# A third arm for experts with 129 to 192 tokens, and another PSUM pool for the third block's transposes

## The chip, the cores and the metric

The kernel runs on one core of one Trainium2 chip. The metric is the device time of one execution in microseconds (us). Before the change it is 526.41 us, the median of three runs (525.23 to 527.89).

## The reference

Three layers follow each other on 1536 tokens of width 512 in float32.

1. Chunked local attention (2 batches, 8 heads, 768 positions, chunks of 32, 8 memory keys).
2. A dense layer pair, `h = x @ w_in`, `g = h * sigmoid(1.702 * h)`, `g @ w_out`, with 2048 inner columns.
3. A mixture of 8 experts, which is the part that the change touches:

```python
logits = x @ w_gate
expert_idx = np.argmax(logits, axis=1)
...
h = np.maximum(np.einsum('ecd,edf->ecf', disp, w1), 0.0)
y = np.einsum('ecf,efd->ecd', h, w2)
...
        out[i] = gate_w[i] * y[expert_idx[i], pos[i]]
```

Each expert has `w1` (512 x 1024) and `w2` (1024 x 512) and takes at most 384 tokens. How many tokens an expert gets depends on the data. With the drawn inputs the experts, in the order in which the kernel takes them, get 224, 291, 128, 160, 128, 256, 160 and 189 tokens; the text calls them expert 0 to expert 7.

## The kernel before

**Precision.** A float32 operand is kept as two numbers, high and low, that TensorE takes at its fast float32 rate (`F32R`). A product is three matmuls: high by high, high by low, low by high. So a weight tile has a high and a low half (`w[:, 0]`, `w[:, 1]`), and activations `xs` and `hT` have too. ScalarE (ACT) writes the high half with a copy, VectorE (DVE) the low half with a subtraction. The weights of the next expert are widened in this way while an expert is computed: a piece is ACT L295 and then DVE L300.

**Control flow.** The program holds all code for every expert one after the other, and branches on the token count in registers; every engine runs the branches for itself. Expert e (from 1 on) goes like this, in `others`:

- The first arm (`both(cnt > P, ...)`, P is 128): `first_of_two` for more than 128 tokens, with the weights stationary and the 256 columns of two token blocks moving, 8 chunks (`fc`) of 12 matmuls in L879; or `first_of(0)` for one block (L962, L971). Both hold the transposes of the next expert's tokens (`next_trans`, L846).
- `thirds_first`: for more than 256 tokens the first layer of a third block, for up to 64 rows in `small_h` (transposes L906, then L918 and L925). All paths hold the first 6 matmuls of layer 2 (`start2`).
- `after_arms`: layer 2 of block 0 (L1002, 24 matmuls with those of `start2`).
- `second`: layer 2 of block 1, either all of it (L1002) or, for up to 192 tokens, `small2` (L940, 16 matmuls on the 64 tokens left, which GpSimd has copied into `hT["pair"]`, L1056); or `second_not`, one small matmul (L1018).

So in the trace 96 matmuls of L879, 24 of L1002 and 16 of L940 in this order are an expert with 129 to 192 tokens. In the code an arm that isn't taken still stands between the others and is jumped over (the branch instructions have the line L1064).

**PSUM.** `psum(kind, name)` takes a buffer from a pool: "t" has 2 buffers, "h" has 4 in the expert stage, and they are reused in turn. A chunk of `first_of_two` takes one "h" buffer, which is free again when DVE has read it (L883).

Of the kernel before, what the change touches and what calls it, by code (L numbers as in the profile page):

```python
# [9 lines left out]
F32 = mybir.dt.float32  # L10
# [5 lines left out]
AF = mybir.ActivationFunctionType  # L16
ALU = mybir.AluOpType
# [4 lines left out]
P = 128  # L22
# [12 lines left out]
PUMPS = (1, 3, 5)  # L35
# [6 lines left out]
KEEPS = (3, 7, 8)  # L42
HALF = P // 2
# [5 lines left out]
TFC = 5  # L49
# [43 lines left out]
def kernel(  # L93
# [14 lines left out]
    nc = tc.nc  # L108
    NT, DM = out.shape
    NG, _, NPAIR, KW = k.shape  # L110
# [3 lines left out]
    E, _, F = w1.shape  # L114
# [5 lines left out]
    KC = DM // P  # L120
# [226 lines left out]
    def w_next(e, keep=KEEP):  # L347

        name, i = (flight[0].name, flight[0].i) if flight else pieces[min(w_at[0], w_end[0] - 1)][:2]
        if not flight or name[1] * 8 + 4 * (name[0] == "w2") + 2 * name[2] + i >= 8 * e + 8 + keep:  # L350
            return False
        w_step()
        w_loads(8 * F // 512)
        return True
# [22 lines left out]
    def w_tile(name, i):  # L377
        while (name, i) not in ready:
            assert flight or wide or w_can_load(), name
            w_pump()  # L380
        return where[name].rearrange("p z (c f) -> p z c f", f=512)
# [22 lines left out]
    def psum(kind, name):  # L404
        pool, tag, shape = ps_pools[kind]
        return pool.tile(shape, F32, tag=tag, name=name)
# [409 lines left out]
    def expert_parts(e, ep, tp, cnt):  # L816
# [15 lines left out]
        def xs_of(b):  # L832

            if b in own:
                return own[b], 0
            i = min(b, 2)
            key = 0 if i < 2 else b
            if key not in xs:
                xs[key] = ep.tile([P, 2, KC, 2 * P if i < 2 else P], F32R, tag="xs" if i < 2 else "xst",
                                  name="xs", bufs=2 if i < 2 else 1)  # L840
            return xs[key], (b * P if i < 2 else 0)

        def trans(b):
            ps = psum("t", "pst")
            for c in range(KC):
                nc.tensor.transpose(ps[:, c * P:(c + 1) * P], xr[b][:, c * P:(c + 1) * P], ident)  # L846
            t, o = xs_of(b)
            hi, lo = t[:, 0, :, o:o + P], t[:, 1, :, o:o + P]
            pv = ps.rearrange("p (c n) -> p c n", n=P)
            act = nc.scalar.activation(out=hi, in_=pv, func=AF.Copy)  # L850
            dve = nc.vector.tensor_tensor(out=lo, in0=pv, in1=hi.bitcast(F32), op=ALU.subtract)
            return act.ins, dve.ins
# [9 lines left out]
        def hT_of(b):  # L862
            key = 0 if b < 2 else b
            if key not in hT:
                hT[key] = ep.tile([P, 2, F2, 2 * P if b < 2 else P], F32R, tag="hT" if b < 2 else "hTt", name="hT", bufs=1)
            return hT[key]
# [32 lines left out]
        def small_h(b):  # L899

            x = narrow(xs_of(b)[0])
            h = narrow(hT_of(b))
            with in_order():
                ps = psum("t", "pst")
                for c in range(KC):
                    nc.tensor.transpose(ps[:, c * HALF:(c + 1) * HALF], xr[b][:HALF, c * P:(c + 1) * P], ident[:HALF, :HALF])  # L906
                pv = ps[:, :KC * HALF].rearrange("p (c n) -> p c n", n=HALF)
                nc.scalar.activation(out=x[:, :, 0], in_=pv, func=AF.Copy)
                nc.vector.tensor_tensor(out=x[:, :, 1], in0=pv, in1=x[:, :, 0].bitcast(F32), op=ALU.subtract)
                start2()  # L910
                hs = []
                for j in range(2):
                    w_tile(("w1", e, j), 0)
                    w = w_tile(("w1", e, j), 1)
                    ps = psum("h", "psh")
                    for wz in range(2):
                        for c in range(KC):
                            nc.tensor.matmul(ps, lhsT=x[:, c].rearrange("p z n -> p (z n)"), rhs=w[:, wz, c, :],  # L918
                                             start=(wz, c) == (0, 0), stop=(wz, c) == (1, KC - 1))
                    hs.append(ep.tile([P, 512], F32, tag="hs", name="hs", bufs=2))  # L920
                    nc.scalar.activation(out=hs[j], in_=ps, func=AF.Copy)
                for j in range(2):
                    ps = psum("h", "psu")
                    for c in range(KC):
                        nc.tensor.matmul(ps[:, c * HALF:(c + 1) * HALF], lhsT=hs[j][:, c * P:(c + 1) * P], rhs=pair,  # L925
                                         start=True, stop=True)
                    hi, lo = (h[:, 4 * j:4 * j + 4, z] for z in range(2))
                    pv = ps[:, :KC * HALF].rearrange("p (c n) -> p c n", n=HALF)
                    nc.scalar.activation(out=hi, in_=pv, func=AF.Relu)
                    nc.vector.scalar_tensor_tensor(out=lo, in0=pv, scalar=0.0, in1=hi.bitcast(F32),  # L930
                                                   op0=ALU.max, op1=ALU.subtract)
# [92 lines left out]
        def next_trans():  # L1024
            if e + 1 < E:
                parts[e + 1].trans(0)
                parts[e + 1].trans(1)

        def steps(part):
            while w_next(e, KEEPS[part]):  # L1030
                pass
# [5 lines left out]
        def first_of(b):  # L1037

            with in_order():
                turn = block_h(b, pump_one)  # L1040
                next_trans()
                turn()
                steps(0)

        def first_of_two():

            for b in range(2, NCB):
                load(b)
            for fc in range(F2):
                mm, act = layer1(fc)  # L1050
                if fc == TFC:
                    after_mm = mm
                if fc in PUMPS:
                    w_next(e, KEEPS[0])
            for z in range(2):
                nc.gpsimd.tensor_copy(hT["pair"][:, :, z], hT_of(0)[:, z, :, P:P + HALF])  # L1056
            with tc.issue_after(after_mm):
                next_trans()
            steps(0)

        def both(cond, yes, no):

            before = w_state()
            with tc.If(cond) as some:  # L1064
                yes()
            after = w_state()
            w_back(before)
            with some.Else():
                no()
            assert w_state() == after  # L1070

        def wide_h(b):
            trans(b)
            start2()
            block_h(b)()

# [72 lines left out]

        def others():  # L1150

            both(cnt[ex] > P, first_of_two, lambda: first_of(0))
            thirds_first()
            after_arms()
            y_of(1)
            both(cnt[ex] > P, second, second_not)
# [308 lines left out]
```

## Time and profile before

| what | value |
|---|---|
| median of three runs | 526.41 us |
| the profiled execution, its own time | 525.63 us |
| its span in the trace | 523.8 us |
| PE (TensorE matmul) busy | 507.5 us, 97% of the span |
| DVE, ACT, POOL (GpSimd) busy | 60%, 52%, 23% |
| share of PE in the chain that ended last | 86% |
| instructions in the trace | 10850, of these 4185 matmuls |
| queue q8, kind instruction | 46 packets, 0.75 MB |
| mean granted TensorE clock | 0.992 |

Times in the trace count from the start of the span. The expert stage takes the last 170 us. A row of the timeline gives start, length, engine, line, operation, output and inputs, how many instructions are merged, and in brackets how long the engine was idle before it and what ended the wait. PEld is the weight load that goes with every matmul; PEldq is the sequencer that hands PE its instructions.

### The profile page before, as it was taken

To read this page: it belongs to the slowest core of one execution; us is meant where nothing else is said; L and a number is where in the kernel's file an instruction comes from. 1 tells how busy PE (TensorE), PEld (TensorE's weight loads), DVE (VectorE), ACT (ScalarE), POOL (GpSimd) and SP (SyncE) were. 2 spreads that over 40 slices of the span, in tenths; PEclk is the share of its full clock that TensorE was granted. 3 is DMA by queue.
4 is the path that set the end of the run, shared out by engine and by line. 5 is a ranking of instruction groups with operands and counts; after the bars stand their busy time and mean duration, and the time that the engine had idled before them with its cause. 6 is when DMAs were issued, how large, how long until landed. Compare 5 with 4: busy or idle time off the path is not lost.

```text
span 523.8 us, 10850 instructions
## 1 busy us (share of the span) xinstructions
PE 507.5 (97%) x4185; PEld 437.7 (84%) x4185; DVE 312.1 (60%) x609; ACT 273.5 (52%) x549; POOL 119.5 (23%) x115
## 2 busy tenths in 40 slices
PE   8899999999999999999999999999999999999994
PEld 3689789889989989989988888778888897889893
DVE  4999894588893283232247444638643976964721
ACT  2798986856662263222255223439553955764520
POOL 3334442333520031000000000053202522521121
PEclk9899999999999999999999999999999999999998
DMA  8898655041440004000048511369734897894010
GB/s 331 291 318 295 205 186 179 1 147 59 167 159 35 0 3 161 0 1 1 0 122 270 173 42 61 124 193 391 284 114 154 253 337 253 297 315 171 25 28 30
DMA packets 38994, 80.90 MB, mean 154 GB/s; under 512 B 3913, under 2 KB 10057, under 8 KB 38922
## 3 DMA queue, kind: packets, MB, share of 16 engines
q1 hardware_dynamic: 36010, 70.66, 39.4%
q0 software_dynamic: 2912, 9.27, 5.5%
q8 instruction: 46, 0.75, 0.6%
q14 instruction: 26, 0.21, 0.1%
HBM read 70.43 MB, written 9.75 MB: 153 GB/s over the span
## 4 chain that ended last, share of the span: by engine, by line
PE 86%; DVE 3%; ACT 3%; issue 3%; DMA 2%; POOL 1%; another core or an unknown queue 0%; SPq 0%; POOLq 0%; DVEq 0%; ACTq 0%
PE acc L590 25%; PE psh L547 25%; PE psy L1002 9%; PE psh L879 9%; PE psh L962 3%; PE pse L505 2%; PE psy L940 2%; PE pss L435 1%; DVE w L300 1%; DMA kt<-in_k_dram 1%; PE psy L779 1%; PE pst L846 1%; PE psr L615 1%; PE psh L763 1%; ACT w L295 1%
## 5 line engine op out<-in xcount | busy, mean ns | idle before, releaser
L547 PEld LDWEIGHTS psh<-xT,w 128*128 128x128 f32 x1152 | 146.9, 188 | 8.8 <-ACT g L566 0.7
L590 PE MATMUL acc<-w,g 128*128 128x512 f32 x576 | 153.0, 400 | 0.0
L547 PE MATMUL psh<-xT,w 128*128 128x256 f32 x1152 | 151.9, 281 | 0.4 <-DVE xT L520 0.2
L590 PEld LDWEIGHTS acc<-w,g 128*128 128x128 f32 x576 | 100.7, 188 | 19.4 <-issue 2.1
L562 ACT ACTIVATE sg<-psh 128x256 f32<-128x256 f32 x96 | 36.8, 384 | 127.7 <-PE psh L547 126.1
L300 DVE TENSOR_TENSOR w<-raw,w 128x1024 fp32r<-128x1024 f32 x64 | 76.1, 1221 | 22.9 <-ACT w L295 20.7
L570 DVE TENSOR_TENSOR g<-sg,g 128x256 fp32r<-128x256 f32 x78 | 37.9, 487 | 80.9 <-ACT g L566 76.7
L295 ACT ACTIVATE w<-raw 128x1024 fp32r<-128x1024 f32 x64 | 65.2, 1055 | 2.3 <-ACTq L1064 1.7
L879 PE MATMUL psh<-xs,w 128*128 128x256 f32 x480 | 58.8, 283 | 0.3 <-DVE hT L883 0.2
L1002 PE MATMUL psy<-w,hT 128*128 128x512 f32 x240 | 57.8, 397 | 0.8 <-ACT xs L850 0.7
L879 PEld LDWEIGHTS psh<-xs,w 128*128 128x128 f32 x480 | 57.6, 189 | 0.9 <-DVE hT L883 0.7
L1002 PEld LDWEIGHTS psy<-w,hT 128*128 128x128 f32 x240 | 44.5, 188 | 11.3 <-issue 1.6
L601 DVE SCALAR_TENSOR_TENSOR x<-acc,x 128x512 f32<-128x512 f32 x36 | 24.1, 685 | 20.8 <-PE acc L590 20.8
L566 ACT ACTIVATE g<-psh 128x256 fp32r<-128x256 f32 x96 | 36.4, 380 | 0.0
L827 POOL DMA_INDIRECT xr<-rows,taker x21 | 29.2, 1391 | 17.8 <-ACTq L1064 10.0
L882 ACT ACTIVATE hT<-psh 128x256 fp32r<-128x256 f32 x40 | 15.0, 382 | 31.6 <-PE psh L879 31.5
L725 POOL DMA_INDIRECT y<-rows,taker x1 | 1.2, 1224 | 123.8 <-DVE cnt_i L732 123.8
L883 DVE SCALAR_TENSOR_TENSOR hT<-psh,hT 128x256 fp32r<-128x256 f32 x40 | 16.2, 420 | 21.1 <-ACT hT L882 21.0
L300 POOL TENSOR_TENSOR w<-w,w 128x512 fp32r<-128x512 f32 x12 | 16.9, 1416 | 42.0 <-ACT w L295 42.0
L290 POOL TENSOR_TENSOR w<-w,rest 128x512 int32<-128x512 int32 x13 | 17.4, 1339 | 35.3 <-DVE w L276 33.6
L295 ACT ACTIVATE w<-w 128x512 fp32r<-128x512 f32 x32 | 19.8, 628 | 9.8 <-POOL w L290 5.0
L276 DVE SCALAR_TENSOR_TENSOR w<-raw,w 128x512 int32<-128x512 int32 x32 | 24.6, 775 | 0.3
(155 smaller groups left out, 568.3 us busy)
## 6 DMA issues: line engine op xcount, KB each, us to landing
raw<-in_w_dram SPq DMA_DIRECT2D x64, 512.0 KB, 6.7
raw<-in_w_out_dram SPq DMA_DIRECT2D x16, 512.0 KB, 4.4
raw<-in_w_in_dram SPq DMA_DIRECT2D x16, 512.0 KB, 3.9
vt<-in_v_dram SPq DMA_DIRECT2D x12, 512.0 KB, 4.7
kt<-in_k_dram SPq DMA_DIRECT2D x12, 368.0 KB, 5.7
qt<-in_q_dram SPq DMA_DIRECT2D x12, 256.0 KB, 5.4
out_dram<-blank SPq DMA_DIRECT2D x12, 256.0 KB, 2.7
rows<-x SPq DMA_DIRECT2D x5, 520.0 KB, 4.8
```

The lines of the kernel that those rows point to most:

```text
L276: nc.vector.scalar_tensor_tensor(out=self.w, in0=self.words()[1], scalar=-0x40000000, in1=self.w, op0=ALU.bitwise_and, op1=ALU.bitwise_or)
L295: nc.scalar.activation(out=w_dst(self.name, self.i, 0), in_=w, func=AF.Copy)
L300: eng.tensor_tensor(out=lo, in0=w, in1=hi.bitcast(F32), op=ALU.subtract)
L547: nc.tensor.matmul(ps, lhsT=w[:, wz, c, i * P:(i + 1) * P], rhs=xT[tb][:, xz, c, :], start=n == 0, stop=n == 3 * KC - 1)
L562: nc.scalar.activation(out=sg_t[u], in_=h_t[u], func=AF.Silu, scale=1.702)
L566: g_last[:1] = [nc.scalar.activation(out=g[:, 0], in_=h_t.pop(u), func=AF.Silu, scale=1.702).ins]
L570: lo = eng.tensor_tensor(out=g[:, 1], in0=sg_t.pop(u), in1=g[:, 0].bitcast(F32), op=ALU.subtract)
L590: nc.tensor.matmul(acc_t[tb][s], lhsT=g[:, gz, s * P:(s + 1) * P], rhs=w[:, wz, wi, :], start=i == 0 and n == 0, stop=u == last_of(k, tb) ...
L601: nc.vector.scalar_tensor_tensor(out=dst, in0=acc_t[tb][s], scalar=1 / 1.702, in1=dst, op0=ALU.mult, op1=ALU.add)
L827: return nc.gpsimd.indirect_dma_start(out=t, out_offset=None, in_=rows[:, :], in_offset=bass.IndirectOffsetOnAxis(ap=taker[:, b, ex:ex + 1 ...
L879: mm = nc.tensor.matmul(ps, lhsT=w[:, wz, c, f0:f0 + P], rhs=t[:, xz, c, :], start=m == 0, stop=m == 3 * KC - 1)
L1002: nc.tensor.matmul(ps, lhsT=h[:, hz, fc, o:o + P], rhs=w[:, wz, fc % 4, :], start=fc == 0 and n == 0, stop=fc == F2 - 1 and n == 2)
```

## The change

A new arm, `first_of_narrow`, is taken for 129 to 192 tokens. Since such an expert has at most 192 rows, the high and the low activations of 192 tokens stand side by side as 384 moving columns: for each chunk and each of 4 contraction blocks one matmul of 384 columns multiplies both by the high weights, and one of 256 columns adds high activations by low weights. That is 64 matmuls in place of 96. (The columns from 192 on of the second one fall on the low part; these rows are rows of zeros there.) The eviction has four steps where there were two: ACT copies the low part, DVE adds the high part, ACT takes the relu, DVE subtracts. `first_of_two` remains for more than 192 tokens, and `first_of(0)` for up to 128, behind a second comparison.

The second edit concerns the transposes of a third block: `small_h` and `wide_h` take their PSUM buffer from "h", no longer from "t".

```diff
--- before.py
+++ after.py
@@ -840,8 +840,8 @@
                                   name="xs", bufs=2 if i < 2 else 1)
             return xs[key], (b * P if i < 2 else 0)
 
-        def trans(b):
-            ps = psum("t", "pst")
+        def trans(b, kind="t"):
+            ps = psum(kind, "pst")
             for c in range(KC):
                 nc.tensor.transpose(ps[:, c * P:(c + 1) * P], xr[b][:, c * P:(c + 1) * P], ident)
             t, o = xs_of(b)
@@ -901,7 +901,7 @@
             x = narrow(xs_of(b)[0])
             h = narrow(hT_of(b))
             with in_order():
-                ps = psum("t", "pst")
+                ps = psum("h", "pst")
                 for c in range(KC):
                     nc.tensor.transpose(ps[:, c * HALF:(c + 1) * HALF], xr[b][:HALF, c * P:(c + 1) * P], ident[:HALF, :HALF])
                 pv = ps[:, :KC * HALF].rearrange("p (c n) -> p c n", n=HALF)
@@ -1052,6 +1052,35 @@
                     after_mm = mm
                 if fc in PUMPS:
                     w_next(e, KEEPS[0])
+            with tc.issue_after(after_mm):
+                next_trans()
+            steps(0)
+
+        def first_of_narrow():
+
+            t, _ = xs_of(0)
+            h = hT_of(0)
+            n = P + HALF
+            for fc in range(F2):
+                w_tile(("w1", e, fc // 4), 0)
+                w = w_tile(("w1", e, fc // 4), 1)
+                f0 = (fc % 4) * P
+                ps = psum("h", "psh")
+                for c in range(KC):
+                    nc.tensor.matmul(ps[:, :2 * n].rearrange("p (z n) -> p z n", z=2), lhsT=w[:, 0, c, f0:f0 + P],
+                                     rhs=t[:, :, c, :n], start=c == 0, stop=False)
+                    mm = nc.tensor.matmul(ps[:, :2 * P], lhsT=w[:, 1, c, f0:f0 + P], rhs=t[:, 0, c, :],
+                                          start=False, stop=c == KC - 1)
+                low = ep.tile([P, 512], F32, tag="hs", name="low", bufs=2)[:, :n]
+                nc.scalar.activation(out=low, in_=ps[:, n:2 * n], func=AF.Copy)
+                nc.vector.tensor_tensor(out=low, in0=ps[:, :n], in1=low, op=ALU.add)
+                nc.scalar.activation(out=h[:, 0, fc, :n], in_=low, func=AF.Relu)
+                nc.vector.scalar_tensor_tensor(out=h[:, 1, fc, :n], in0=low, scalar=0.0, in1=h[:, 0, fc, :n].bitcast(F32),
+                                               op0=ALU.max, op1=ALU.subtract)
+                if fc == TFC:
+                    after_mm = mm.ins
+                if fc in PUMPS:
+                    w_next(e, KEEPS[0])
             for z in range(2):
                 nc.gpsimd.tensor_copy(hT["pair"][:, :, z], hT_of(0)[:, z, :, P:P + HALF])
             with tc.issue_after(after_mm):
@@ -1070,7 +1099,7 @@
             assert w_state() == after
 
         def wide_h(b):
-            trans(b)
+            trans(b, "h")
             start2()
             block_h(b)()
 
@@ -1149,7 +1178,8 @@
 
         def others():
 
-            both(cnt[ex] > P, first_of_two, lambda: first_of(0))
+            both(cnt[ex] > P + HALF, first_of_two,
+                 lambda: both(cnt[ex] > P, first_of_narrow, lambda: first_of(0)))
             thirds_first()
             after_arms()
             y_of(1)
```

What the program of an engine holds now is shown by the order of its instructions, at three places. The first is PE, expert 3 (160 tokens), from the end of expert 2 on; `psh` is a chunk's PSUM buffer, `w_97` and `w_96` the two tiles of `w1`, `xs` the activations. Before:

```order
L1064 UNCONDITIONAL_BRANCH
L1018 LDWEIGHTS ones
L1018 MATMUL psy<-ones 32x8
L1064 UNCONDITIONAL_BRANCH
L1064 COMPARE_AND_BRANCH
L879 MATMUL psh<-xs,w_97 128x256 x48
L879 MATMUL psh<-xs,w_96 128x256 x48
L846 MATMUL pst<-ident,xr 128x128 x8
L1064 UNCONDITIONAL_BRANCH
```

And now, with the first of the 64 rows of the new arm (384 and 256 columns in turn):

```order
L1093 COMPARE_AND_BRANCH
L879 MATMUL psh<-xs,w_97 128x256 x48
L879 MATMUL psh<-xs,w_96 128x256 x48
L846 MATMUL pst<-ident,xr 128x128 x8
L1093 UNCONDITIONAL_BRANCH
L1093 COMPARE_AND_BRANCH
L1070 MATMUL psh<-xs,w_97 128x384
L1072 MATMUL psh<-xs,w_97 128x256
```

Where expert 3 fell through one comparison into L879, it now jumps over 104 matmuls to a second comparison and falls into the new arm there.

The second place is the end of that arm, again on PE, where the arm of 128 tokens begins. Now:

```order
L1070 MATMUL psh<-xs,w_96 128x384
L1072 MATMUL psh<-xs,w_96 128x256
L846 MATMUL pst<-ident,xr 128x128 x8
L1093 UNCONDITIONAL_BRANCH
L962 MATMUL psh<-w_97,xs 128x512 x12
L962 MATMUL psh<-w_96,xs 128x512 x6
L971 MATMUL psu<-ident,hs 128x128 x4
L962 MATMUL psh<-w_96,xs 128x512 x6
L846 MATMUL pst<-ident,xr 128x128 x8
L971 MATMUL psu<-ident,hs 128x128 x4
L1093 UNCONDITIONAL_BRANCH
L1093 COMPARE_AND_BRANCH x2
```

The 72 matmuls of the new arm stand between `first_of_two` and `first_of`, in each of the experts 1 to 7 (64 in expert 7, which has no transposes): an expert with 128 tokens makes two jumps in a row at its start, and one with more than 192 jumps further at the end of its arm.

The third place is DVE in the new arm; `low` is the buffer of the added halves, L300 a piece of the next expert's weights:

```order
L1093 COMPARE_AND_BRANCH
L300 TENSOR_TENSOR w_94<-raw_0_3362,w_94 128x1024
L300 TENSOR_TENSOR w_94<-raw_1_3363,w_94 128x1024
L1076 TENSOR_TENSOR low<-psh,low 128x192 x2
L300 TENSOR_TENSOR w_4519<-raw_2_3364,w_4519 128x1024
L1078 SCALAR_TENSOR_TENSOR hT<-low,hT 128x192 x2
L1076 TENSOR_TENSOR low<-psh,low 128x192 x2
L1078 SCALAR_TENSOR_TENSOR hT<-low,hT 128x192 x2
```

Where L883 stood once for a chunk, an addition and a subtraction stand now, in pairs of chunks, and the addition is what frees the PSUM buffer.

## Rows read from the trace of the kernel before

**Rows 1.** The page, parts 1 and 2: the span and PE.

```profile
span 523.8 us, 10850 instructions
...
PE 507.5 (97%) x4185; PEld 437.7 (84%) x4185; DVE 312.1 (60%) x609; ACT 273.5 (52%) x549; POOL 119.5 (23%) x115
```

**Rows 2.** Timeline of PE in the expert stage, experts 2 to 6.

```profile
399.49 4.35 PE L962 MATMUL psh<-w,xs 128*128 128x512 f32 x18
...
412.90 5.96 PE L879 MATMUL psh<-xs,w 128*128 128x256 f32 x48
419.06 5.96 PE L879 MATMUL psh<-xs,w 128*128 128x256 f32 x48 [0.20 <-DVE hT L883]
...
431.31 3.89 PE L940 MATMUL psy<-w,hp 128*128 128x512 f32 x16
435.82 4.41 PE L962 MATMUL psh<-w,xs 128*128 128x512 f32 x18 [0.62 <-issue]
...
463.00 11.27 PE L1002 MATMUL psy<-w,hT 128*128 128x512 f32 x48 [0.70 <-ACT xs L850]
...
474.31 11.66 PE L879 MATMUL psh<-xs,w 128*128 128x256 f32 x96
485.80 1.04 PE L846 MATMUL pst<-ident,xr 128*128 128x128 f32 x8
486.59 5.82 PE L1002 MATMUL psy<-w,hT 128*128 128x512 f32 x24
492.26 3.89 PE L940 MATMUL psy<-w,hp 128*128 128x512 f32 x16
```

**Rows 3.** Timeline of DVE at the start of expert 3.

```profile
411.77 6.90 DVE L300 TENSOR_TENSOR w<-raw,w 128x1024 fp32r<-128x1024 f32 x6 [0.27 <-DVEq L1064]
...
418.59 0.75 DVE L883 SCALAR_TENSOR_TENSOR hT<-psh,hT 128x256 fp32r<-128x256 f32 x2
```

**Rows 4.** Branches by line, whole and in four windows: count, min/median/max ns, first to last.

```profile
L1064 PEldq COMPARE_BRANCH  x43: 65/190/4550, 357.6 to 512.6; - x43
...
L1064 PEldq COMPARE_BRANCH  x2: 179/1862/3546, 395.3 to 395.6; - x2
...
L1064 PEldq COMPARE_BRANCH  x3: 181/318/4550, 430.0 to 431.1; - x3
...
L1064 PEldq COMPARE_BRANCH  x2: 187/1284/2380, 460.1 to 460.3; - x2
...
L1064 PEldq COMPARE_BRANCH  x1: 326/326/326, 505.5 to 505.5; - x1
```

**Rows 5.** The page, part 3: the queue that loads code (packets, MB, share).

```profile
q8 instruction: 46, 0.75, 0.6%
```

**Rows 6.** Windows: 208.8 to 337.9, from one packet of q8 to the seventh after.

```profile
208.80:337.90 129.10, 128.96 (x891) 111.58 (x889) 53.51 (x154) 44.04 (x109) 1.22 (x1) 1.00 0.25 81
```

**Rows 7.** DMA queues in 433.2 to 433.3, 439 to 439.1, 506.6 to 506.7: packets begun.

```profile
q8 instruction: 1, 0.02, 58.8%
...
q8 instruction: 1, 0.02, 62.9%
...
q8 instruction: 1, 0.02, 85.6%
```

**Rows 8.** Windows: span, busy by engine (PE, PEld, DVE, ACT, POOL), clock, DMA share, GB/s.

```profile
430.00:439.00 9.00, 8.38 (x37) 6.50 (x36) 5.76 (x8) 2.70 (x6) 1.18 (x1) 1.00 0.95 328
453.00:465.00 12.00, 11.19 (x85) 10.43 (x85) 8.57 (x14) 6.61 (x15) 4.42 (x5) 1.00 1.01 377
478.00:512.00 34.00, 34.00 (x232) 31.39 (x231) 17.85 (x33) 13.46 (x30) 7.13 (x9) 1.00 0.12 36
```

**Rows 9.** Timeline of expert 1, start of its third block.

```profile
377.98 0.43 PE L906 MATMUL pst<-ident,xr 64*128 64x64 f32 x4 [1.17 <-DVE xs L851]
...
379.80 0.42 DVE L909 TENSOR_TENSOR xs<-pst,xs 128x256 fp32r<-128x256 f32 x1
...
380.27 3.99 PE L918 MATMUL psh<-w,xs 128*128 128x512 f32 x16 [0.28 <-DVE xs L909]
```

## The prediction, made before the changed kernel ran

> **What bounds the kernel now.** I read the page first: PE is busy for 507.5 of 523.8 us [rows 1], so what happens to PE's work, or to its few gaps, sets the time. The profiled execution took 525.63 us, 0.8 below the median of the runs (526.41); sums are made against 525.63 and carried over to the median. A difference under 0.5% (2.6 us) can't be told from none, since the three runs of the kernel before lie 2.7 us apart.
>
> Then I read PE's timeline in the expert stage. Three experts have 96 matmuls of L879, 24 of L1002 and 16 of L940 (experts 3, 6 and 7; the rows show 3 and 6) and will take the new arm [rows 2]. Experts 1 and 5 keep the wide arm, 2 and 4 the arm of 128. PE is idle there in only three places: 0.20 us before the second half of expert 3's chunks, 0.62 at the start of expert 4, 0.70 in expert 5 [rows 2].
>
> Who ends these waits decides the forecast, so I looked at PE's sequencer. Of 43 branches half take 0.19 us or less [rows 4], but four take 2.4 to 4.6: in expert 2's start 3.55, in expert 4's start 4.55, in expert 5 at 460.3 2.38 [rows 4], and a fourth in expert 4, of 3.04, that no row here shows. The second and third end just before PE's idle times of 0.62 and 0.70: 431.1 + 4.55 is 435.7, and PE begins at 435.82; 460.3 + 2.38 is 462.7, and PE begins at 463.00 [rows 2, 4]. So the 0.70 that the timeline puts down to ACT L850 was a jump.
>
> These four wait for code. Queue q8 brings 46 packets [rows 5]; over 7 of them PE ran 891 matmuls and 889 weight loads, 254 instructions a packet [rows 6]. So code comes in blocks of about 256 instructions. For the jump in expert 4's start a packet begins at 433.2, and PE's sequencer goes on at 435.7, 2.4 us later [rows 4, 7]. The next packet begins at 439.0 [rows 7], 3.4 us after the sequencer has come into that block. So a block is asked for when the one before it is entered, and can be run 3.4 + 2.4 = 5.8 us later. With idle DMA queues it is faster: the branch at 505.5 ends at 505.8, a packet begins at 506.6 [rows 4, 7], so 0.8 + 2.4 = 3.2 us. The DMA engines' share is 0.95 and 1.01 in such stretches of the weights' loads, 0.12 after 478 [rows 8]. Counted along the order in steps of 256, one offset puts the four slow jumps, and no other, into a block asked for too late. [...]
>
> Most of that time is hidden: the jump at 431.1 stands in the code behind 16 matmuls of L940, which begin on PE only at 431.31 [rows 2, 4]. The sequencer runs some 16 matmuls ahead, 3.8 us at 512 columns and 1.9 at 256.
>
> **What the new arm removes.** [...] A chunk of the contraction goes from 3 x 119.7 = 359 to 178 + 120 = 298 ns, 32 of them from 11.49 to 9.53 us. That is 1.96 an arm, 5.9 us for three; with 384 at 120 ns 11.5, at 236 ns 0.3.
>
> **What it adds in evictions.** Two operations on DVE and two on ACT for a chunk, where there was one on each. DVE's were 0.75 for two [rows 3], on 256 columns; at that price (an upper bound for 192) two take 0.75 us on either engine, below PE's 1.19 a chunk. The PSUM buffer is freed by the addition, as early as L883 did. The chain of four ends about 0.8 us later than two did, before layer 2 of block 0 (5.7 us [rows 2]) asks for the last chunks or L940 for `hp`; nothing on the path, 0 to 0.3. If that cover were gone it would be 0.8 for each of three arms. At expert 3's start DVE works on L300 until 418.6 [rows 3]: if the arm began at 412.90 as now, the fifth chunk would be due at 412.90 + 4 x 1.19 = 417.7 and still come at 419.06, and that arm would save only some 0.8 us.
>
> **The third block's transposes.** Only expert 1 runs them. L906 waits 1.17 us for a "t" buffer, but the next wait stands behind it: L918 starts at 380.27 when DVE's L909 ends (379.80 + 0.42) [rows 9], and that one waits for weights on ACT and DVE, not for L906. Earlier transposes make a longer wait there: 0 (a gain of at most 0.3 if L909 moved too).
>
> **What it adds in code.** An expert's code grows by 72 matmuls, by the order from some 330 to 400, so from 2.8 to 3.4 blocks, and the jumps grow or double. Placing the blocks in the new order with the same offset:
>
> - Expert 2: two jumps in a row. The first target is loaded, the second's block is asked for at 395.5 and there at 398.7 to 401.3. PE could start at 399.49 [rows 2]. I take 400.0: 0.5 us (0 to 1.9).
> - Expert 3: the last jump of expert 2 enters a block that is there at about 412, and the new arm starts just past that block's end. So its code is asked for at 412 and there 3.2 to 5.8 us later, nearer to the latter with the loads running: 417.4. PE is free at 413.4. I take 4.0 us (0 to 5.1). By then DVE has caught up, so the 0.20 us before the fifth chunk goes, and the arm saves its full 1.96.
> - Expert 4: one more boundary, some 14 matmuls into its arm: 1.0 us (0 to 2.3).
> - Expert 5: at the end of its arm the jump over two arms enters a new block at 460.1, and the next jump leaves it at once. Its code is there at 465.9; L1002 starts at 466.1 in place of 463.00 [rows 2]: 3.1 us (0.3 to 3.1).
> - Expert 6: a boundary a few matmuls into the new arm: 0.7 us (0 to 1.0). Expert 7: idle queues, 0.
>
> Sum: 9.3 us lost, 5.9 + 0.2 = 6.1 won. 525.63 + 3.2 = 528.8 for a profiled execution, 529.6 us for the median.
>
> **The rivals.**
>
> *Code in time: faster.* If a block can be run within about 4 us of being asked for, the jumps stay hidden behind PE's queue. It decides at about 5 us: 0.8 less than 5.8 counts twice in expert 3, where two loads follow each other, once in expert 5 and some 0.5 in the others, so that the loss is 6.4 and about the gain. For it: 39 of 43 branches are quick, and q8 has a share of only 0.6% [rows 5]. Against it: the 5.8 us at 435.7. Then only expert 3's start keeps its wait for DVE, and the gain is 0.8 + 2 x 1.96 = 4.7, less 0.1: 521.8 us for the median. [...]
>
> *384 columns at the price of 512.* If the split rows or the overlapping sums cost the middle matmul its rate, the arms win nothing and the loads remain: 526.4 + 9.3 - 0.5 = 535 us. Nothing in the trace shows such a pattern, so nothing speaks for it but that.
>
> *Gain and loss cancel.* The expert stage's loads follow the weights' widening; if expert 3's code comes at 415 instead of 417.4, the loss is 6.9 against 6.1 won, and the time 527.2.
>
> **How the numbers follow.** Late code outweighing the matmuls: 0.55. Code in time: 0.27. Cancelling: 0.10. 384 at 512's price: 0.08. For the likeliest, the bounds of its terms give 525 to 534. Since 527.0 to 529.0 still lies within 0.5%, I give it 0.35 slower and 0.20 the same; code in time gives 0.24 faster, 0.03 the same; cancelling 0.01 faster, 0.07 the same, 0.02 slower; the last 0.01 the same, 0.07 slower. Together 0.25, 0.31, 0.44. The range reaches into the rival's case, from 521.5, and to 534.0 above.
>
> **What would show it.** In the trace after: L1070 and L1072 in turn, 64 to an arm, about 298 ns a pair; PE idle for several us before the first L1070 of expert 3 and before the first L1002 of expert 5, put down to "issue" or to some engine long done; branches of more than 2 us at more than four places; about 50 packets of q8. It is wrong if PE runs through expert 3's start without a gap, if a pair takes 350 ns, or if PE waits inside the arms for DVE's additions.

## The result and the profile after

The changed kernel takes 532.99 us (median of 4 runs, 531.82 to 533.75), the kernel before 526.63 beside it (4 runs): ratio 1.0119, interval 1.0093 to 1.0145. It is slower by 6.4 us; the forecast was 3.2, at 529.6 us. The mechanism was the forecast one, code that comes too late; what it costs beyond the gain of the arms is twice the forecast. The profiled execution took 531.82 us.

The page of the changed kernel, parts 1 and 3 (against [rows 1, 5]):

```profile
span 530.0 us, 10749 instructions
...
PE 505.2 (95%) x4085; PEld 434.9 (82%) x4089; DVE 317.6 (60%) x633; ACT 279.0 (53%) x573; POOL 113.6 (21%) x108
...
q8 instruction: 50, 0.82, 0.6%
```

PE is busy only 2.3 us less, with 96 matmuls fewer (by the weight loads, 4185 to 4089; four matmul records are missing in the trace), and the span is 6.2 us longer. So PE waits more, and it works more slowly somewhere. PE's timeline in experts 1 to 6 of the changed kernel (against [rows 2]) shows where:

```profile
394.95 3.90 PE L940 MATMUL psy<-w,hT 128*128 128x512 f32 x16
400.02 4.42 PE L962 MATMUL psh<-w,xs 128*128 128x512 f32 x18 [1.17 <-DVE y L943]
...
413.50 0.44 PE L1070 MATMUL psh<-xs,w 128*128 128x384 f32 x1
417.63 0.58 PE L1072 MATMUL psh<-xs,w 128*128 128x256 f32 x1 [3.69 <-issue]
418.01 0.52 PE L1070 MATMUL psh<-xs,w 128*128 128x384 f32 x1
...
420.67 0.34 PE L1070 MATMUL psh<-xs,w 128*128 128x384 f32 x1
...
421.27 0.33 PE L1070 MATMUL psh<-xs,w 128*128 128x384 f32 x1
421.44 0.28 PE L1072 MATMUL psh<-xs,w 128*128 128x256 f32 x1
421.55 0.33 PE L1070 MATMUL psh<-xs,w 128*128 128x384 f32 x1
...
463.69 1.03 PE L846 MATMUL pst<-ident,xr 128*128 128x128 f32 x8
469.09 14.11 PE L1002 MATMUL psy<-w,hT 128*128 128x512 f32 x48 [4.37 <-issue]
```

Two gaps stand out: 3.69 us at the first matmuls of expert 3's new arm, 4.37 ahead of expert 5's layer 2. Behind each, the same matmuls take longer: the 48 of L1002 14.11 us, where they took 11.27 [rows 2]. The windows of the changed kernel (span, PE, PEld, DVE, ACT, POOL, granted clock, DMA share, GB/s) say why:

```profile
417.63:420.50 2.87, 2.87 (x11) 2.87 (x12) 1.87 (x3) 0.59 (x2) 0.28 (x1) 0.50 0.99 354
420.50:428.10 7.60, 7.60 (x54) 7.60 (x53) 5.11 (x14) 4.63 (x14) 0.00 (x0) 0.99 1.05 393
...
469.09:474.70 5.61, 5.61 (x13) 4.43 (x14) 3.50 (x3) 2.95 (x3) 0.00 (x0) 0.50 0.62 202
474.70:483.20 8.50, 8.50 (x37) 6.64 (x35) 1.45 (x3) 1.82 (x4) 1.01 (x1) 0.97 0.64 207
```

Behind both gaps the granted clock is 0.50, and 0.99 and 0.97 in the windows that follow, from 420.5 and 474.7 on. PE had been idle for 3.69 and 4.37 us. Whether that is the cause these rows don't show; for expert 5 the filler experiment below does.

The branches on PE's sequencer (count, min/median/max ns, first to last; against [rows 4]), whole, at expert 2's start and at expert 5's layer 2:

```profile
L1093 PEldq COMPARE_BRANCH  x48: 65/218/5942, 356.7 to 518.8; - x48
...
L1093 PEldq COMPARE_BRANCH  x1: 4555/4555/4555, 395.2 to 395.2; - x1
...
L1093 PEldq COMPARE_BRANCH  x2: 293/3118/5942, 462.5 to 462.9; - x2
```

The third line is the jump behind the 4.37: a branch from 462.9 to 468.8, and PE starts at 469.09. The 1.17 us that the timeline puts down to "DVE y" is a branch too, 395.2 + 4.56 = 399.8. As in [rows 4, 7], a packet of q8 stands in the stall. It begins at 466.3, and the branch ends 2.5 us later:

```profile
q8 instruction: 1, 0.02, 34.8%
```

That is the row of q8 for 466.2 to 466.4; a window from 460 to 466.2 has none. From entering the block to running it: 468.8 - 462.9 = 5.9 us (forecast 5.8).

Expert 3's gap stands behind no long branch. The last long branch ahead of it began at 409.7 and ended at 412.1, and the next packet of q8 begins inside the gap, at 415.3 (the second row is that of q8 for 415.2 to 415.4; a window from 410 to 415.2 has none):

```profile
L1093 PEldq COMPARE_BRANCH  x1: 2428/2428/2428, 409.7 to 409.7; - x1
...
q8 instruction: 1, 0.02, 30.6%
```

PE goes on at 417.63, 2.3 us behind the start of the packet and 5.5 us behind the end of that branch. The forecast had this code asked for at 412 and there at 417.4.

The table gives the time from the first matmul of one step to that of the next, worked out from PE's starts in four traces. The last two are experiments below: the changed kernel with 80 (the repeated run) and with 48 matmuls that never run.

| stretch on PE | before | changed | with 80 | with 48 |
|---|---|---|---|---|
| expert 1, L846 to L918 | 4.50 | 4.50 | 5.42 | 5.52 |
| expert 2's start, L940 to L962 | 3.73 | 5.07 | 3.73 | 4.04 |
| expert 2, L1002 to expert 3's arm | 5.82 | 5.84 | 5.80 | 11.87 |
| expert 3's arm | 11.96 | 14.65 | 11.12 | 10.66 |
| expert 3, L846 to L1002 | 0.79 | 0.79 | 1.56 | 0.79 |
| expert 3, L1002 to expert 4's L962 | 10.17 | 9.39 | 10.34 | 12.43 |
| expert 5, L846 to L1002 | 1.74 | 5.40 | 1.26 | 5.36 |
| expert 5, its 48 of L1002 | 11.31 | 14.15 | 12.01 | 12.86 |
| expert 6's arm | 11.50 | 9.96 | 9.97 | 9.88 |
| expert 6, L846 to L1002 | 0.79 | 0.79 | 1.79 | 0.79 |
| expert 7's arm, to L1002 | 11.46 | 10.06 | 9.77 | 9.77 |
| first L962 of the stage to the last matmul | 166.65 | 173.87 | 166.23 | 178.78 |

The stage is 7.2 us longer in the changed kernel; it began 0.95 earlier in that trace, which makes the span's 6.2.

### The profile page after: what moved, and what is told of

Same layout as the page of the kernel before. It is cut to its first block, busy times and chain, and to the rows that moved or that the text cites. A ratio compares the mean times of both kernels' runs of the same rounds, so it can differ in the third digit from the quotient of the medians.

```text
span 530.0 us, 10749 instructions
## 1 busy us (share of the span) xinstructions
PE 505.2 (95%) x4085; PEld 434.9 (82%) x4089; DVE 317.6 (60%) x633; ACT 279.0 (53%) x573; POOL 113.6 (21%) x108
## 5 line engine op out<-in xcount | busy, mean ns | idle before, releaser
L300 DVE TENSOR_TENSOR w<-raw,w 128x1024 fp32r<-128x1024 f32 x64 | 76.0, 1221 | 29.7 <-ACT w L295 25.8
L1002 PE MATMUL psy<-w,hT 128*128 128x512 f32 x240 | 60.9, 412 | 5.0 <-issue 5.0
L1002 PEld LDWEIGHTS psy<-w,hT 128*128 128x128 f32 x240 | 46.5, 197 | 16.6 <-issue 5.7
L827 POOL DMA_INDIRECT xr<-rows,taker x18 | 24.4, 1358 | 33.9 <-ACTq L1093 18.8
L1072 PE MATMUL psh<-xs,w 128*128 128x256 f32 x96 | 27.8, 290 | 3.7 <-issue 3.7
L1070 PE MATMUL psh<-xs,w 128*128 128x384 f32 x96 | 30.0, 351 | 0.0
L300 POOL TENSOR_TENSOR w<-w,w 128x512 fp32r<-128x512 f32 x12 | 16.8, 1403 | 42.2 <-ACT w L295 42.2
L265 ACT ACTIVATE w<-raw 128x512 f32<-128x512 f32 x32 | 21.3, 676 | 6.6 <-DMA raw<-in_w_out_dram 5.8
L1012 POOL DMA_INDIRECT out_dram<-y,taker x10 | 12.2, 1224 | 56.0 <-ACT y L1011 32.9
```

Of the source, the lines that this page charges most:

```text
L300: eng.tensor_tensor(out=lo, in0=w, in1=hi.bitcast(F32), op=ALU.subtract)
L827: return nc.gpsimd.indirect_dma_start(out=t, out_offset=None, in_=rows[:, :], in_offset=bass.IndirectOffsetOnAxis(ap=taker[:, b, ex:ex + 1 ...
L1002: nc.tensor.matmul(ps, lhsT=h[:, hz, fc, o:o + P], rhs=w[:, wz, fc % 4, :], start=fc == 0 and n == 0, stop=fc == F2 - 1 and n == 2)
L1070: nc.tensor.matmul(ps[:, :2 * n].rearrange("p (z n) -> p z n", z=2), lhsT=w[:, 0, c, f0:f0 + P], rhs=t[:, :, c, :n], start=c == 0, stop=False)
L1072: mm = nc.tensor.matmul(ps[:, :2 * P], lhsT=w[:, 1, c, f0:f0 + P], rhs=t[:, 0, c, :], start=False, stop=c == KC - 1)
```

## The experiments

The theory: the new code moves the jumps against blocks of about 256 instructions (254 a packet [rows 6]), some then wait for a block, and the clock falls behind the long gaps (to 0.50 in the windows above). The rivals: the new arm's evictions or matmuls cost the time, or the second edit does.

**One edit alone: the second.**

```diff
-        def trans(b):
-            ps = psum("t", "pst")
+        def trans(b, kind="t"):
+            ps = psum(kind, "pst")
...
-                ps = psum("t", "pst")
+                ps = psum("h", "pst")
...
-            trans(b)
+            trans(b, "h")
```

> The kernel before with the second edit alone (the third block's transposes take an h buffer); the new arm is left out. Late-code theory: nothing is added to the code, and in expert 1 the wait only moves from the transposes behind them to the copy that DVE makes, so 526.6 us, the same within 0.5%. Rival (the edit itself costs, because the h buffers that it takes are missing for the next chunk): 528 or more, with a wait of PE inside expert 1's third block of over 1 us more than before.

528.41 us, ratio 1.0033 (1.0012 to 1.0053): within the 0.5% that was called the same, though with 2.0 us over the runs beside it not quite nothing. PE's timeline of this run:

```profile
360.62 5.84 PE L1002 MATMUL psy<-w,hT 128*128 128x512 f32 x24 [1.32 <-issue]
...
382.57 4.00 PE L918 MATMUL psh<-w,xs 128*128 128x512 f32 x16 [1.49 <-DVE xs L909]
...
490.04 5.86 PE L1002 MATMUL psy<-w,hT 128*128 128x512 f32 x24 [0.99 <-issue]
```

The wait in expert 1's third block moved behind L906 and kept its size, 1.49 us where it was 1.17 + 0.28 [rows 9]; the rival's wait of over 1 us more didn't come there. Two waits are new, 1.32 us ahead of expert 0's layer 2 and 0.99 in expert 6. Both stand behind no engine, "issue" as with the late jumps, and packets of q8 begin 2.4 and 2.2 us ahead of their ends (358.2 and 487.9). Why these blocks came later than in the kernel before isn't shown.

**The code without its saving.** The two comparisons are exchanged, so that no expert takes the new arm, and `first_of_two` gets back the GpSimd copies that the change had moved into the new arm:

```diff
+            for z in range(2):
+                nc.gpsimd.tensor_copy(hT["pair"][:, :, z], hT_of(0)[:, z, :, P:P + HALF])
...
-            both(cnt[ex] > P + HALF, first_of_two,
-                 lambda: both(cnt[ex] > P, first_of_narrow, lambda: first_of(0)))
+            both(cnt[ex] > P, first_of_two,
+                 lambda: both(cnt[ex] > P + HALF, first_of_narrow, lambda: first_of(0)))
```

> The changed kernel's code, with all three arms in it, but the two comparisons exchanged, so that every expert with more than 128 tokens runs first_of_two, and the new arm is never run: the code without its saving. Late-code theory: PE's work is that of before, and jumps again reach code that was asked for too late. Expert 2's start 1.3 us as in the changed kernel, expert 5's layer 2 about 4.4 us of idle and some 2.8 of half clock as in the changed kernel, and expert 3's late code now not at its arm's start but at its layer 2, some 4.3 us and half clock behind it; 1 to 2 us in expert 6. In all 540 us (535 to 545). Rival (the new arm's own matmuls or evictions cost what was lost, code that isn't run is free): 526.6 to 527.

540.31 us, ratio 1.0262 (1.0207 to 1.0317). PE runs the 4185 matmuls of before. Its timeline shows the gaps where they were expected:

```profile
433.35 7.38 PE L1002 MATMUL psy<-w,hT 128*128 128x512 f32 x24 [4.33 <-issue]
...
475.04 12.87 PE L1002 MATMUL psy<-w,hT 128*128 128x512 f32 x48 [4.29 <-issue]
...
502.23 5.82 PE L1002 MATMUL psy<-w,hT 128*128 128x512 f32 x24 [1.75 <-ACT w L295]
```

24 of L1002 take 7.38 us behind 4.33 idle and 5.82 behind 1.75. The time is 13.9 us over that of the kernel before, though the new arm is never run; the second edit, which is in it too, was 2.0 alone. So the rival falls, by which the new arm's matmuls or evictions cost what was lost.

**Never-run matmuls ahead of expert 1, in the changed kernel and in the kernel before.** Only the place of the later code changes.

```diff
         def others():
+            if e == 1:
+                with tc.If(cnt[ex] > NCB * P):
+                    for _ in range(80):
+                        nc.tensor.matmul(y_of(1)[:CH, :8], lhsT=ones[:, :CH], rhs=ones[:, :8], start=True, stop=True)
```

> The changed kernel with 80 small matmuls more (160 instructions on PE) in an arm that no expert takes, ahead of expert 1: what is run is the same, only the later code stands 160 instructions further on against the blocks of 256. Late-code theory: the jumps at expert 3's start and at expert 5's layer 2 then fall within blocks that are there; the gaps of 3.7 and 4.4 us go, and the half clock behind them; about 2 us of idle come at expert 1's arm's end, under 1 us in experts 5 and 6. 523 us (520 to 526), which is faster than the kernel before. Rival (dead code only costs, or the gaps come from an engine or buffer): 533 or a little more, gaps where they are.

526.02 us, ratio to before 0.9997 (0.9969 to 1.0026): 7 us less than the changed kernel, 3 more than expected. The gaps of 3.69 and 4.37 are gone. The added comparison cost 0.73 us of idle ahead of expert 1, and expert 3's arm got a wait of 1.39 for DVE, shown below. A further 0.33 ahead of expert 0's layer 2 isn't the comparison's: the kernel below that has the same matmuls and no added comparison has it too. Of the 2 us expected at the end of expert 1's arm 1.42 came. With 40 of them in the kernel before:

> The kernel before with 40 small matmuls more (80 instructions on PE) in an arm that no expert takes, ahead of expert 1; the work that is run is the same. Late-code theory: a jump at expert 1's first matmuls and one at expert 3's layer 2 now reach blocks asked for too late: some 4 us idle at about 366 us, some 2 at about 428, the waits at expert 4's start and in expert 5 shrink; 532 us (530 to 535, the upper end if the clock falls behind the long gap). Rival (code that isn't run is free): 526.6 to 527.

529.11 us, ratio 1.0043 (1.0022 to 1.0064): the sign was right, half the size. The one late jump that came is in the timeline:

```profile
429.90 7.25 PE L1002 MATMUL psy<-w,hT 128*128 128x512 f32 x24 [2.27 <-ACTq L1064]
```

2.27 us idle, and the 24 matmuls behind it take 7.25 us against 5.82. The 4 us at expert 1 didn't come: a packet of q8 begins at 362.4, ahead of the expert's first matmul at 365.5, where I had counted it later.

**Filler matmuls in expert 5's gap.** They tell whether layer 2 was slow because PE had been idle.

```diff
+            if e == 5:
+                one = nc.const_aps.tensor(1.0, (P, 1), BF16)
+                for _ in range(18):
+                    nc.tensor.matmul(y_of(0), lhsT=one.to_broadcast([P, P]), rhs=one.to_broadcast([P, 512]), start=True, stop=True)
             thirds_first()
```

> The changed kernel with 18 matmuls of 512 bf16 columns (236 ns each at full clock, 4.2 us) put in expert 5 alone, behind its arm's jump and ahead of the comparison for the third block. They are pure filler: PE works on them while it would be idle for 4.37 us, and the code behind the comparison should come when it did. If idleness lowers the clock: layer 2 (L1002, 48 matmuls) begins at the same time, within 0.5 us, and takes 11.3 us again in place of 14.11, so the span is 2 to 3 us shorter, less up to 1 us that the 36 instructions may cost expert 6 by shifting its code: 531 us. Rival (layer 2 is slow there for another reason, as the weights' loads or the first run of new code): it takes 14 us again, 533 to 534 us.

531.29 us, ratio to before 1.0078 (1.0053 to 1.0103), 1.7 below the changed kernel's median. The timeline, and the window of layer 2:

```profile
467.06 4.10 PE L1186 MATMUL psy<-const-bfloat16-1.0 128*128 128x512 bf16 x17
...
471.45 11.29 PE L1002 MATMUL psy<-w,hT 128*128 128x512 f32 x48 [0.29 <-issue]
```

```profile
471.45:482.70 11.25, 11.25 (x49) 8.93 (x49) 4.95 (x6) 4.78 (x7) 1.02 (x1) 1.00 0.77 246
```

Layer 2 begins as long after the transposes as in the changed kernel (5.26 against 5.40 us), so the code came no sooner, but it takes 11.29 us at a clock of 1.00. So idleness was the cause of the 2.8 us in expert 5.

**Both arms in the new form**, without and with never-run matmuls:

```diff
         def first_of_two():
             for b in range(2, NCB):
                 load(b)
-            for fc in range(F2):
-                mm, act = layer1(fc)
...
+            first_of_pairs(2 * P)
```

> The changed kernel with first_of_two written in the new form too (512 and 256 columns in place of three times 256; two more eviction steps), which leaves 64 instructions less in every expert's code and moves the blocks. On PE the form is worth nothing (236 + 119.7 against 359 ns). Late-code theory: in place of 1.2, 3.7 and 4.4 us idle at expert 2's start, expert 3's start and in expert 5, about 0, 2.0 and 2.3 (in expert 5 also since the 16 matmuls queued ahead of its jump last 2.8 us and not 1.9), and less half clock: 526.5 us (524 to 529). Rival (the gaps come from the new arms' evictions): four arms and more with them, 535 or more.

532.02 us, ratio 1.011 (1.0079 to 1.0142): a miss by 5.5 us. Timeline, and the two branches from 411.5 to 414 us:

```profile
379.57 0.43 PE L906 MATMUL pst<-ident,xr 64*128 64x64 f32 x4 [2.85 <-ACT ex L856]
...
420.26 0.66 PE L1065 MATMUL psh<-xs,w 128*128 128x384 f32 x1 [4.63 <-DVE w L300]
```

```profile
L1089 PEldq COMPARE_BRANCH  x2: 1980/4056/6133, 411.7 to 413.8; - x2
```

Further on PE's timeline (from 467 to 481 us) has one more gap of over 1 us, inside expert 5's layer 2:

```profile
471.39 9.48 PE L1002 MATMUL psy<-w,hT 128*128 128x512 f32 x40 [1.39 <-issue]
```

The count of blocks had put about 2 us at expert 3's start and 2.3 in expert 5. The first came as 4.63, the second as 1.39 (a packet of q8 begins at 469.0, 2.4 us ahead of its end), and one of 2.85 came in expert 1. The time is nearer to the rival's 535 than to the forecast, but the rival's place is wrong: once an arm has begun, PE waits in it for at most 0.39 us. The 4.63 ends just behind a branch of 6.13 us (413.8 to 420.0), whatever the releaser's name says: late code again, of a larger size.

> Both arms in the new form and 104 small matmuls that no expert runs, inside the arm of expert 0 that is jumped over anyway. Late-code theory: idle of about 2 us at expert 3's start with some half clock behind it, none of over 1 us in experts 2, 4, 5, 6 and 7: 524.5 us (522.5 to 526.5). Rival: as the kernel with both arms in the new form and no such matmuls.

534.95 us, ratio 1.0157 (1.0104 to 1.021): a miss by 10. Its timeline, and the two branches from 417 to 425 us:

```profile
358.91 2.37 PE L962 MATMUL psh<-w,xs 128*128 128x512 f32 x6 [2.81 <-issue]
...
384.97 0.66 PE L906 MATMUL pst<-ident,xr 64*128 64x64 f32 x4 [3.55 <-ACT w L295]
...
427.89 0.66 PE L1065 MATMUL psh<-xs,w 128*128 128x384 f32 x1 [6.06 <-DVE w L300]
```

```profile
L1089 PEldq COMPARE_BRANCH  x2: 3354/4790/6225, 417.9 to 421.4; - x2
```

As expected, no gap longer than 1.00 us stands in experts 2 and 4 to 7. The gap at expert 3 was expected at 2 and is 6.06: the branches of 3.35 and 6.23 us follow each other, so two blocks in a row come late. Gaps that weren't expected are the 2.81 in expert 0, behind the never-run matmuls, and the 3.55 in expert 1. The count finds most places, but not the sizes.

**Never-run matmuls inside an arm that is jumped over anyway.** The kernel with 80, the kernel with 48, the kernel before with 68, and the first of these again:

```diff
             with tc.If(cnt[E] < P) as some:
+                with tc.If(cnt[ex] > NCB * P):
+                    for _ in range(80):
+                        nc.tensor.matmul(y_of(1)[:CH, :8], lhsT=ones[:, :CH], rhs=ones[:, :8], start=True, stop=True)
```

> The changed kernel with the same 80 small matmuls that no expert runs, but inside an arm of expert 0 that is jumped over anyway, so no further comparison is run ahead of expert 1. Late-code theory: the gaps at expert 3's start (3.7) and in expert 5 (4.4) stay away, and the idle of 0.33 and 0.73 us ahead of expert 1 that came with the comparison goes: 525 us (523.5 to 526.5). Rival (where dead code stands doesn't matter, only how much there is): 533.

> The changed kernel with 48 in place of 80 small matmuls that no expert runs, in the same arm of expert 0. Nothing that is run differs, and there is less dead code than in the kernel of 80. Late-code theory: counted in blocks of 256 this is the worst place: 2 us or more idle at expert 3's start, some 3.6 at its layer 2, 2.3 in expert 4, over 4 in expert 5, and half clock behind each: 539 us (536 to 543), 14 more than with 80. Rival (the amount of dead code counts, or the position doesn't): 525 to 533.

With 80: 525.06 us, ratio 0.9986 (0.9964 to 1.0008). With 48: 538.76, ratio 1.0244 (1.0186 to 1.0303). Work and arms are the same and the dead code is less, yet 13.7 us lie between them (12.9 to the repeated run with 80, which ran beside the one with 48). Of the idle that was to go with the comparison, the 0.33 us stayed, and the 0.73 is down to 0.06. The kernel with 48 in its timeline:

```profile
421.67 0.66 PE L1070 MATMUL psh<-xs,w 128*128 128x384 f32 x1 [5.97 <-DVE w L300]
...
445.54 4.41 PE L962 MATMUL psh<-w,xs 128*128 128x512 f32 x18 [2.03 <-DVE y L944]
...
476.34 12.66 PE L1002 MATMUL psy<-w,hT 128*128 128x512 f32 x48 [4.33 <-issue]
```

Three of the four places are those expected (expert 3's start, experts 4 and 5); at expert 3's layer 2 there is only 0.67, and its start has 5.97 where 2 or more was expected. The half clock expected behind each gap didn't come behind the 2.03: the 18 of L962 take 4.41 us, as before [rows 2].

> The kernel before with 68 small matmuls that no expert runs, in the arm of expert 0 that is jumped over: the best place that the count of blocks gives for it. Late-code theory: its 0.62 us at expert 4's start and 0.70 in expert 5 go, nothing else changes: 1.3 us less than the kernel before, 525.6 us (524.5 to 526.6). It is the measure against which the new arm at its best place is to be set. Rival: as before, 526.9.

526.36 us, ratio 1.0012 (0.9987 to 1.0037): no gain that can be measured. Expert 5's 0.70 is gone, expert 4's 0.62 is 0.40.

> The changed kernel with 80 small matmuls in expert 0's arm once more, in more rounds and beside the kernel before at its own best place. 525.1 us, and faster than the kernel before by 1 to 3 us; against the kernel before at its best place 0 to 1.5 us faster: in its trace the three arms and what follows them up to layer 2 are worth 0.2, 1.0 and 1.3 us.

525.83 us, ratio 0.9992 (0.9966 to 1.0019): 0.5 us under the kernel before at its best place, and no measurable gain over the kernel before, where 1 to 3 us were expected. DVE's timeline at expert 3's start, and PE's:

```profile
411.11 6.90 DVE L300 TENSOR_TENSOR w<-raw,w 128x1024 fp32r<-128x1024 f32 x6 [0.26 <-DVEq L1093]
417.93 0.61 DVE L1076 TENSOR_TENSOR low<-psh,low 128x192 f32<-128x192 f32 x2
```

```profile
418.33 0.44 PE L1070 MATMUL psh<-xs,w 128*128 128x384 f32 x1 [1.36 <-DVE low L1076]
```

With the code there in time, expert 3's fifth chunk waits 1.36 us for a buffer that DVE frees only behind six pieces of L300.

**ACT empties the buffer.** This is the kernel with 80 and one more edit:

```diff
-                low = ep.tile([P, 512], F32, tag="hs", name="low", bufs=2)[:, :n]
-                nc.scalar.activation(out=low, in_=ps[:, n:2 * n], func=AF.Copy)
-                nc.vector.tensor_tensor(out=low, in0=ps[:, :n], in1=low, op=ALU.add)
+                two = ep.tile([P, 512], F32, tag="hs", name="low", bufs=2)
+                low = two[:, :n]
+                nc.scalar.activation(out=two[:, :2 * n], in_=ps[:, :2 * n], func=AF.Copy)
+                nc.vector.tensor_tensor(out=low, in0=low, in1=two[:, n:2 * n], op=ALU.add)
```

> As the run before it, but in the new arm ACT copies all 384 columns out of the PSUM buffer, and DVE adds the two halves in SBUF, so that the buffer no longer waits for DVE. If the 1.38 us idle ahead of expert 3's fifth chunk is DVE's old work (L300 until 418.7) holding that buffer: the fifth and sixth chunk start on time, the seventh may still wait, since the two SBUF buffers of the sums wait for DVE too: 0 to 1.2 us less, 524.7 us. Rival (the wait has another cause, as ACT's queue): ACT has more to do and the time is 525.1 or up to 1 us more.

525.43 us, ratio 0.9999 (0.9973 to 1.0026). The arm begins at 415.64 here, and its second, third and fourth chunk at 416.91, 418.06 and 419.20, so 1.15 us apart. PE's timeline has the fifth chunk and the one wait in the arm, at the seventh; ACT's has the copy that frees the buffer for the seventh:

```profile
420.35 0.33 PE L1070 MATMUL psh<-xs,w 128*128 128x384 f32 x1
...
423.87 0.45 PE L1070 MATMUL psh<-xs,w 128*128 128x384 f32 x1 [1.06 <-ACT low L1076]
```

```profile
423.32 0.49 ACT L1076 ACTIVATE low<-psh 128x384 f32<-128x384 f32 x1 [1.04 <-DVE hT L1079]
```

The fifth and sixth chunk start on time (420.35 and 421.50) and the seventh waits, as expected: ACT's copy stands 1.04 us for DVE's subtraction. The wait for DVE moved two chunks on, from 1.36 to 1.06 us. The arm takes 10.78 us against 11.12, too little for the median to tell.

## Why the prediction was right in kind and wrong in size

**Right.** With 384 columns a pair takes 421.55 - 421.27 = 0.28 us at a granted clock of 0.99 (window from 420.5; forecast 298 ns). The 5.9 us in the sum rest on 119.7 ns for 256 columns, (485.80 - 474.31) / 96 in [rows 2], and on 178 ns for 384 columns, which no row of the kernel before shows: an estimate, the middle between that and the (492.26 - 486.59) / 24 = 236 ns of 512 columns [rows 2]. In the changed kernel a matmul of 384 columns takes 421.44 - 421.27 = 0.17 us. The two large gaps came where they were forecast and from the forecast cause: 3.69 us at expert 3's start (forecast 4.0; its code was there at 417.6, forecast 417.4) and 4.37 in expert 5 (forecast 3.1 on top of 0.70). From entering a block to running it took 5.9 us at a DMA share of 0.85 (from 462.9 to 468.8; forecast 5.8), and q8 brought 50 packets (about 50). The third block's transposes bring nothing in the changed kernel, 4.50 us from L846 to L918 as before. The side remark held that expert 3's arm would save only 0.8 us if it began on time: 11.96 - 11.12 = 0.84 with 80.

**The step that failed** is the sum of late code: its terms are idle times alone. I wrote "3.1 us" for expert 5 and "4.0" for expert 3, and had no term for the clock behind the gap. It cost 14.11 - 11.27 = 2.8 us in expert 5. In expert 3 five pairs from 418.01 to 420.67 took 2.66 us where 5 x 0.28 is 1.4, about 1.2 too long. That is 4.0 together, as much as the stage was missed by (7.2 against 3.2). The filler experiment shows for expert 5 that idleness is its cause; for expert 3 the granted clock of 0.50 behind its gap says the same, without an experiment of its own.

**Mis-sized, and nearly cancelling by luck.** Expert 2's start lost 1.34 (0.5); expert 5's gap 0.6 more than forecast; expert 4 won 1.0 (0.78 at its start, 0.26 in its first arm) in place of losing 1.0, its old 0.62 gone with the new place of the code; expert 6's boundary cost nothing visible (0.7). The arms won 1.54 and 1.40 in experts 6 and 7, and in expert 3 14.65 - 3.69 - 1.2 = 9.8, so 2.2: 5.1 in all, not 6.1. The evictions, put at 0 to 0.3 us, may be part of this: in expert 7 PE is idle for 0.43 us ahead of layer 2, which it wasn't before, and layer 2 takes 5.84 us where it took 5.58. What ended that idle time isn't shown.

**Signs and sums.** One sign didn't come: branches of more than 2 us at more than four places. There are three (4.56 at 395.2, 2.43 at 409.7, 5.94 at 462.9), and expert 3's gap is behind none, since the arm runs into the late block behind its first matmul, without a jump. The lower bound of 525 us doesn't follow from the terms: their lower bounds sum to 0.3 us, which with 6.1 won is 520.6 us. The upper bounds, 13.4 us, do give 534.

**The rivals.** *Code in time* can be looked at in the kernel with 80: 525.1 to 525.8, not 521.8. Its three arms do save 0.84 + 1.53 + 1.69 = 4.1 us, but 0.77 and 1.00 come back between L846 and L1002 of experts 3 and 6, and 0.9 ahead of expert 1's L906. These are late code still, whatever engine the timeline names: branches of 2.40 (from 422.1), 2.69 (from 482.7) and 4.10 us (from 373.5) end 0.3 us ahead of PE's next matmul. Expert 6's is this one:

```profile
L1093 PEldq COMPARE_BRANCH  x1: 2688/2688/2688, 482.7 to 482.7; - x1
```

So that run doesn't have its code in time, and the rival's condition, a block run within about 4 us, fails in the changed kernel with 5.5 and 5.9 us. That late jumps can be placed out of the way altogether was not shown: the 80 matmuls removed the large gaps only, and the 104, with both arms in the new form, made it worse. *Gain and loss cancel* asked for expert 3's code at 415; it came at 417.6. *384 columns at the price of 512* falls with the 0.28 us.

## What to carry to other kernels

Code that is never run wasn't free here, where jumps cross it (525.06 us with 80 such matmuls, 538.76 with 48): ask, for every taken jump, whether its target's block had been asked for early enough (5.9 us from entering it to running it in the changed kernel's expert 5), and how much queued work PE has to cover the wait (of a branch of 4.55 us 0.62 was left as idle time [rows 2, 4], of one of 5.94 us 4.37). Add to every forecast gap on PE what the clock takes behind it (2.8 us behind the 4.37). A change to a branchy kernel of this kind is measured together with the place of its code, which alone moved the time by some 13 us here; to judge the edit itself, compare several places.

## What the runs showed of the hardware that was not expected

Behind every idle time of PE of 2.8 us and more in the expert stage of these traces the matmuls took longer: six of L962 2.37 us behind 2.81, where six take 1.64 in the changed kernel, and the 48 of L1002 14.11 behind 4.37, at a granted clock of 0.50. Behind those of 1.84 and less they never did: six of L1002 took 1.66 us behind 1.84 (the first run with 80). In between it went both ways, at the same place. Ahead of expert 1's L906 there are three cases, told apart by the six matmuls of L1002 that follow: the repeated run with 80 (1.66 us), the run with 48 (2.38), and the run with ACT's copies (2.93):

```profile
377.83 0.43 PE L906 MATMUL pst<-ident,xr 64*128 64x64 f32 x4 [2.52 <-ACT w L295]
378.20 1.66 PE L1002 MATMUL psy<-w,hT 128*128 128x512 f32 x6
...
379.27 0.43 PE L906 MATMUL pst<-ident,xr 64*128 64x64 f32 x4 [1.94 <-ACT w L295]
379.63 2.38 PE L1002 MATMUL psy<-w,hT 128*128 128x512 f32 x6
...
378.42 0.66 PE L906 MATMUL pst<-ident,xr 64*128 64x64 f32 x4 [2.42 <-ACT w L295]
379.00 2.93 PE L1002 MATMUL psy<-w,hT 128*128 128x512 f32 x6
```

In the run with 48 the granted clock was 0.50 from 380.3 to 383.6. At expert 4's start 18 of L962 took 4.41 us behind 2.03 us of idle time (with 48), as in [rows 2], and 5.97 behind 1.97 (ACT's copies). So the length of the idle time alone didn't decide it there.

A late block's price is no constant: the longest branches took 5.9 to 6.2 us, and where two late blocks follow each other PE stood for 5.97 and 6.06 us. In the five waits whose packet is timed above (two in the changed kernel, two with the second edit alone, one with both arms in the new form) it was 2.2 to 2.8 us from the start of the packet to PE's next matmul. What varies more is the time until the packet begins: in the changed kernel 3.2 us in expert 3 and 3.4 in expert 5, against the 0.8 that the prediction read with idle queues.
